# 64 bytes in place of 128 in front of x, g and their sums

## The chip, the core and the metric

The kernel runs on one core of a Trainium2 chip. The metric is the device time of one execution in microseconds (us). One execution was also taken by the profiler; its rows are the evidence for what follows. Engines are named as in the profile: PE is TensorE's matmuls, PEld its weight loads, DVE is VectorE, ACT is ScalarE, SP the engine that issues the transfers.

## What is computed

A pooled attention followed by a feed-forward layer, all in float32. The 576 keys and values of each head are averaged over groups of 8 to 72; eight batches of eight heads with a width of 64 give 4608 tokens of 512 numbers.

```
k_p = k.reshape(B, H, Sp, 8, D).mean(axis=3)      # v_p likewise
scores = q @ k_p.T / sqrt(D);  attn = softmax(scores)
x = (attn @ v_p)  -> (4608, 512)
h = x @ w_in                                       # 512 x 2048
g = max(h, 0) + log1p(exp(-abs(h)))                # softplus
out = g @ w_out                                    # 2048 x 512
```

## The kernel before

The tokens are worked through in 18 chunks of 256 (`CT`). A chunk's attention yields `x`, held as a rounded part `xh` and the rest `xl`, both of type float32r. The weights `w_in` and `w_out` stay in the core's memory (tiles `w0` to `w15`), also as a rounded part and a rest. Each product of two numbers is then three float32r matmuls: high by high, high by low, low by high.

**First product (line 494, `h`).** Per block of 128 columns of `w_in`, 12 matmuls: a 128x128 piece of `w` is loaded as the weights, and 256 tokens of `x` stream through it. In the steady part two blocks (a unit `u` of eight) make 24 matmuls in a row.

**Softplus and its parts.** ACT writes `g` (line 543, 499 in the early chunks) and its rounded part `gh` (557); DVE writes the rest `gl` (564) and, from chunk 4 on, sums of quarters of `g` (594 to 597), which ACT and DVE split into the two halves of `so` (608, 613).

**Second product.** Chunks 0 to 3 accumulate in `acc` (lines 516 and 576): a piece of `gh` or `gl` is the weights and 512 columns of `w` stream. From chunk 4 on (line 684, `m`) seven products take the place of eight: a piece of `gh`, `gl` or `so` is the weights and 256 columns of `w` stream, 21 matmuls a unit. So `x` streams over loads of `w`, and `w` streams over loads of `g`'s parts. The steady part alternates 24 of `h` with 21 of `m`.

The order of all work is written out by a planner in the kernel (`Order`), from costs that the program states; it knows names of slots, not addresses or sizes of tiles. Slots `G0` to `G5`, `o0`, `o1` hold `g`, `sf`, `pm`, output rows and, in chunk 3, `gh` and `gl`, as they come free.

**Where tiles stand.** Tiles of a pool are laid one behind the other in the order in which their tags are first used. `pe` (line 402), the attention weights of the last 8 keys as DVE writes them (line 406), uses `6 * R` of its columns (`R` is 32) and is `7 * R` wide: the last 32 columns, 128 bytes a partition, are never touched. Everything laid behind it is shifted by that width. In the program as built before the change, bytes in a partition:

```
tile (tag)                                  begins   modulo 256   size
vs0, vs1, vlo0, vlo1                          4544 .. 8640     192
w0 .. w15                                  10688 .. 133568   192   8192 each
loads of k, v and weights, q, kp, qT, E     141760 .. 170944   192
G0 (pm, g, sf, o, gh, gl)                   175040             192   2048
pe                                          177088             192    896
lt_, pT                                     177984, 180032      64
x (X01, X23)                                184128, 195904      64   8192 each
gh, gl (two each)                           192320 .. 209216    64   1536 each
so (two)                                    210752, 214848      64   4096 each
G1, G2 and o0, o1, G3 (named by place)      193856 .. 227136    64   2048 each
mn, sm (two each)                           229184 .. 229280    64, 96, 128, 160   32 each
ident                                         1152             128    512
```

All pieces that matmuls read begin a multiple of 512 bytes behind their tile's start, so a tile's phase modulo 256 is that of each of its pieces. `G0` stands ahead of `pe`, the other `G` slots behind it: work in `G0` has the phase of the weights, the same work in another slot the phase of `x`. In unit 3 of chunk 3 the planner put `gh` in `G0` (and `gl` in a slot behind `pe`); in units 0 to 2, 4, 6 and 7 of that chunk both are behind `pe`.

Of the kernel before, what the change touches and what calls it, by code (L numbers as in the profile page):

```python
# [9 lines left out]
F32 = mybir.dt.float32  # L10
# [93 lines left out]
def pooled_attention_softplus_ffn(  # L104
# [14 lines left out]
    P = 128  # L119
# [19 lines left out]
    one = ctx.enter_context(tc.tile_pool(name="one", bufs=1))  # L139
# [157 lines left out]
    R = 4 * KL  # L297
# [31 lines left out]
    class Tile:  # L329
# [69 lines left out]

        def ends(self):  # L400

            pe = one.tile([P, 7 * R], F32, tag="pe", name="pe")
            self.pe = pe[:, 0:6 * R].rearrange("p (a n r) -> p a n r", a=2, n=3)
            for a in range(2):
                hs = slice(4 * a, 4 * a + 4)
                nc.vector.tensor_tensor(  # L406
                    out=self.pe[:, a].rearrange("p n (h j) -> p n h j", h=4),
                    in0=e_[self.c][:, self.t, hs, KM:SP].unsqueeze(1).to_broadcast([P, 3, 4, KL]),
                    in1=self.sm[:, hs].unsqueeze(1).unsqueeze(3).to_broadcast([P, 3, 4, KL]),
                    op=ALU.mult)  # L410
# [539 lines left out]
    def attend(c):  # L950
# [15 lines left out]
        for t, x in enumerate(tiles):  # L966
# [7 lines left out]
            q_free[c, t] = o  # L974
            o = op(ACT, act(512), lambda x=x, s=s_q: x.qT_out(s.tile), [o], [s_q, s_qT])
            ends, ss = [], [Slot("bank"), Slot("bank")]
            p = op(PE, 0.7, lambda x=x, ss=ss: x.scores([bank(s, "sc") for s in ss]), [o, *keys],
                   [s_qT, *ss])
# [18 lines left out]
            if c < N1:  # L997
                exps.extend(ends)
            else:
                subs += ends  # L1000
            norms.append((x, ends, s_E, s_sm, s_pm, s_pe))
        if c == N1:
            ex = op(ACT, 1.2, lambda: exponential(e_[c]), subs, table="exp")
# [386 lines left out]
```

## Time and profile before

| | |
|---|---|
| median of 3 runs | 928.23 us (927.97 to 931.43) |
| the profiled execution | 930.85 us, of which its span 929.1 us |
| PE busy | 904.6 us (97%) |
| PEld busy | 859.6 us |
| DVE, ACT busy | 648.6 us, 407.3 us |
| granted TensorE clock, mean | 0.994 |

The span is from the first instruction to the last. A busy PE says little of its pace, since matmuls overlap and one that takes 281 ns is followed by the next after about 118: the pace of a run is read from the starts of its first matmul and of the next run's first, divided by the count.

### The profile page before, as it was taken

How to read it: one execution, taken by the hardware profiler on the slowest of the kernel's cores; microseconds unless marked ns; L12 is line 12 of the kernel's file. 1: busy time of each engine (PE TensorE's matmuls, PEld its weight loads, DVE VectorE, ACT ScalarE, POOL GpSimd, SP SyncE). 2: the span in 40 equal slices, each digit the busy share in tenths (PEclk: the TensorE clock that was granted, in tenths of full speed). 3: DMA queues.
4: the chain of work that ended last, by engine and by line, in shares of the span. 5: the costliest groups of instructions: out<-in, count | busy, mean ns of one | idle time of the engine just before them, and what ended most of it. 6: DMA issues, size and time to landing. Idle time of an engine off the chain costs nothing.

```text
span 929.1 us, 20504 instructions
## 1 busy us (share of the span) xinstructions
PE 904.6 (97%) x8304; PEld 859.6 (93%) x8304; DVE 648.6 (70%) x1600; ACT 407.3 (44%) x824; POOL 2.4 (0%) x19
## 2 busy tenths in 40 slices
PE   4899999999999999999999999999999999999997
PEld 2678989889899999999999999999999999999997
DVE  4799988868876767777777755777666565747454
ACT  4755433344443534544453435353535344434332
POOL 1000000000000000000000000000000000000000
PEclk9899999999999999999999999999999999999999
DMA  8974636544898678788668865777656566647472
GB/s 231 259 249 147 205 106 182 167 150 136 289 276 239 225 212 256 201 248 233 224 198 248 238 208 186 212 245 214 220 172 216 182 206 186 222 141 227 158 238 78
DMA packets 107085, 191.12 MB, mean 206 GB/s; under 512 B 46064, under 2 KB 60400, under 8 KB 106992
## 3 DMA queue, kind: packets, MB, share of 16 engines
q1 hardware_dynamic: 106992, 189.82, 66.2%
q8 instruction: 65, 1.06, 0.5%
q14 instruction: 28, 0.23, 0.1%
HBM read 167.25 MB, written 22.54 MB: 204 GB/s over the span
## 4 chain that ended last, share of the span: by engine, by line
PE 93%; DVE 3%; DMA 3%; ACT 0%; issue 0%; SPq 0%; DVEq 0%; ACTq 0%
PE h L494 43%; PE m L684 30%; PE acc L516 7%; PE sc L357 3%; PE acc L576 2%; PE avp L461 2%; PE qTp L337 2%; PE avp L468 1%; PE ptp L420 1%; DMA vst<-in_v_dram 1%; PE ltp L432 1%; PE kps L921 1%; DMA kvst<-in_k_dram 1%; DMA kvl<-in_v_dram 1%; DMA wst<-in_moe_w_in_dram 0%
## 5 line engine op out<-in xcount | busy, mean ns | idle before, releaser
L494 PE MATMUL h<-x,w 128*128 128x256 f32 x3456 | 437.8, 282 | 0.7 <-DVE w L822 0.7
L494 PEld LDWEIGHTS h<-x,w 128*128 128x128 f32 x3456 | 422.5, 188 | 4.0 <-DVE w L822 0.9
L543 ACT ACTIVATE g<-h 128x512 f32<-128x512 f32 x120 | 71.7, 598 | 287.0 <-PE h L494 284.7
L684 PE MATMUL m<-w,so 128*128 128x256 f32 x1344 | 177.7, 281 | 0.0
L684 PEld LDWEIGHTS m<-w,so 128*128 128x128 f32 x1344 | 167.4, 188 | 0.0
L684 PE MATMUL m<-w,gh 128*128 128x256 f32 x672 | 133.4, 288 | 0.0
L594 DVE TENSOR_TENSOR sf<-g 128x128 f32<-128x128 f32 x112 | 32.7, 292 | 141.1 <-ACT g L543 140.0
L684 PEld LDWEIGHTS m<-w,gh 128*128 128x128 f32 x672 | 102.2, 188 | 1.9
L684 PE MATMUL m<-w,gl 128*128 128x256 f32 x336 | 94.1, 280 | 0.0
L608 ACT CAST so<-sf 128x512 fp32r<-128x512 f32 x112 | 69.6, 621 | 55.1 <-DVE sf L597 54.6
L613 DVE TENSOR_TENSOR so<-sf,so 128x512 fp32r<-128x512 f32 x112 | 77.3, 690 | 21.9 <-ACT so L608 21.8
L564 DVE TENSOR_TENSOR gl<-g,gh 128x384 fp32r<-128x384 f32 (+1 forms) x120 | 67.3, 560 | 0.7 <-ACT gh L557 0.5
L684 PEld LDWEIGHTS m<-w,gl 128*128 128x128 f32 x336 | 63.1, 188 | 0.0
L516 PE MATMUL acc<-w,g 128*128 128x512 f32 x192 | 60.7, 397 | 0.5 <-ACT g L499 0.5
L557 ACT ACTIVATE gh<-h 128x384 fp32r<-128x384 f32 (+1 forms) x120 | 59.3, 494 | 0.0
L499 ACT ACTIVATE g<-h 128x256 fp32r<-128x256 f32 x96 | 31.6, 382 | 60.7 <-PE h L494 55.6
L705 DVE TENSOR_TENSOR o<-o,m 128x256 f32<-128x256 f32 x98 | 39.7, 418 | 3.9 <-ACT o L697 1.0
L516 PEld LDWEIGHTS acc<-w,g 128*128 128x128 f32 x192 | 34.2, 189 | 6.6 <-ACT g L499 0.7
L364 DVE TENSOR_REDUCE mn<-sc 128x4 f32<-128x288 f32 x72 | 31.1, 450 | 12.2 <-PE sc L357 12.1
L516 PE MATMUL acc<-w,gl 128*128 128x512 f32 x96 | 38.0, 396 | 0.0
L597 DVE TENSOR_TENSOR sf<-g,sf 128x128 f32<-128x128 f32 x112 | 32.7, 292 | 3.9
L406 DVE TENSOR_TENSOR pe<-E,sm 128x96 f32<-128x96 f32 x72 | 15.2, 252 | 26.9 <-PE ltp L432 26.9
(165 smaller groups left out, 933.0 us busy)
## 6 DMA issues: line engine op xcount, KB each, us to landing
w<-wi SPq DMA_DIRECT2D x224, 512.0 KB
out_dram<-o SPq DMA_DIRECT2D x36, 256.0 KB
q<-in_q_dram SPq DMA_DIRECT2D x32, 256.0 KB
wst<-in_moe_w_in_dram SPq DMA_DIRECT2D x32, 256.0 KB
wst<-in_moe_w_out_dram SPq DMA_DIRECT2D x16, 512.0 KB
wi<-w SPq DMA_DIRECT2D x16, 512.0 KB
kst<-in_k_dram SPq DMA_DIRECT2D x24, 288.0 KB
vst<-in_v_dram SPq DMA_DIRECT2D x24, 256.0 KB
```

The lines of the kernel that those rows point to most:

```text
L494: nc.tensor.matmul(out=ps[:, 0:CT], lhsT=row(w, kc), rhs=x[:, kc], start=first and kc == j == 0, stop=last and kc == KC - 1 and j == 2)
L499: nc.scalar.activation(out=g, in_=ps[:, 0:CT], func=AF.Softplus)
L516: nc.tensor.matmul(out=accs[c][t], lhsT=a[:, ts], rhs=w, start=f == 0 and j == 0, stop=f == FC - 1 and j == 2)
L543: nc.scalar.activation(out=g, in_=x.rearrange("p (b i) -> p b i", i=P), func=AF.Softplus)
L557: nc.scalar.activation(out=gh, in_=quarters(c, x.rearrange("p (b i) -> p b i", i=P)), func=AF.Softplus)
L564: nc.vector.tensor_tensor(out=gl, in0=quarters(c, g), in1=gh.bitcast(F32), op=ALU.subtract)
L594: tt(out=sf[:, 2], in0=g[:, 0], in1=g[:, 2], op=ALU.add)
L597: tt(out=sf[:, 3], in0=g[:, 3], in1=sf[:, 1], op=ALU.subtract)
L608: nc.scalar.copy(out=so[:, 0], in_=ss[c, u])
L613: nc.vector.tensor_tensor(out=so[:, 1], in0=sf, in1=so[:, 0].bitcast(F32), op=ALU.subtract)
L684: nc.tensor.matmul(out=ms[c][n], lhsT=x, rhs=y, start=u == 0 and j == 0 and n in (1, 6, 5, 4), stop=u == FP - 1 and j == 2 and n in (2, 7, ...
L705: nc.vector.tensor_tensor(out=o, in0=in0, in1=m[n], op=how)
```

## The change

The tile `pe` is made 6 R + 16 columns wide in place of 7 R: 832 bytes a partition in place of 896, with the used columns as they were.

```diff
         def ends(self):
 
-            pe = one.tile([P, 7 * R], F32, tag="pe", name="pe")
+            pe = one.tile([P, 6 * R + 16], F32, tag="pe", name="pe")
             self.pe = pe[:, 0:6 * R].rearrange("p (a n r) -> p a n r", a=2, n=3)
```

Everything behind `pe` moves down by 64 bytes: `x`, `gh`, `gl`, `so`, `pT`, `lt_` and the `G` slots but `G0` from 64 to 0 modulo 256; `mn` and `sm` from 64, 96, 128, 160 to 0, 32, 64, 96. What stands ahead of it stays, the weights at 192 and `G0` at 192 among it. No instruction is added, removed or resized.

## Rows read from the trace of the kernel before

**Rows 1.** The page: span, busy time of each engine, and the chain that ended last.
```profile
span 929.1 us, 20504 instructions
PE 904.6 (97%) x8304; PEld 859.6 (93%) x8304; DVE 648.6 (70%) x1600; ACT 407.3 (44%) x824; POOL 2.4 (0%) x19
PE 93%; DVE 3%; DMA 3%; ACT 0%; issue 0%; SPq 0%; DVEq 0%; ACTq 0%
```

**Rows 2.** PE's groups by form: line, tiles, shape, count | busy us, mean ns.
```profile
L494 PE MATMUL h<-x,w 128*128 128x256 f32 x3456 | 437.8, 282 | 0.7 <-DVE w L822 0.7
L684 PE MATMUL m<-w,so 128*128 128x256 f32 x1344 | 177.7, 281 | 0.0
L684 PE MATMUL m<-w,gh 128*128 128x256 f32 x672 | 133.4, 288 | 0.0
L684 PE MATMUL m<-w,gl 128*128 128x256 f32 x336 | 94.1, 280 | 0.0
```

**Rows 3.** The chain in order of time: start us, us, what; runs of h, m.
```profile
255.46 2.84 PE h L494 x24
258.30 2.49 PE m L684 x21
260.79 2.84 PE h L494 x24
263.64 2.49 PE m L684 x21
266.13 2.84 PE h L494 x24
```

**Rows 4.** Timeline of PE, chunk 3's unit 3, gh in G0: start us, us, what.
```profile
224.21 0.49 PE L420 MATMUL ptp<-ident,pm 128*128 128x128 f32 x3
224.46 0.71 PE L576 MATMUL acc<-w,gh 128*128 128x512 f32 x2
225.00 0.39 PE L576 MATMUL acc<-w,gl 128*128 128x512 f32 x1
225.23 0.62 PE L576 MATMUL acc<-w,gh 128*128 128x512 f32 x2
...
227.07 0.40 PE L576 MATMUL acc<-w,gl 128*128 128x512 f32 x1
227.31 0.27 PE L432 MATMUL ltp<-ident,pe 128*96 128x128 f32 x1
```

**Rows 5.** Timeline of PE, chunk 3's unit 7, gh and gl behind pe.
```profile
252.51 0.63 PE L576 MATMUL acc<-w,gh 128*128 128x512 f32 x2
252.97 0.39 PE L576 MATMUL acc<-w,gl 128*128 128x512 f32 x1
...
255.30 0.75 PE L494 MATMUL h<-x,w 128*128 128x256 f32 x5
```

**Rows 6.** Timeline of PE: first and last of the 73 joins m to h.
```profile
260.51 0.28 PE L684 MATMUL m<-w,gl 128*128 128x256 f32 x1
260.63 0.63 PE L494 MATMUL h<-x,w 128*128 128x256 f32 x4
...
916.18 0.28 PE L684 MATMUL m<-w,gl 128*128 128x256 f32 x1
916.30 0.51 PE L494 MATMUL h<-x,w 128*128 128x256 f32 x3
```

**Rows 7.** Weight loads by form, and transposes by line: durations min/median/max.
```profile
L684 PEld LDWEIGHTS m<-w,so x1344: 187/188/193, 258.7 to 923.6; 128*128 128x128 f32 x192
L420 PEld LDWEIGHTS ptp<-ident,pm x144: 138/141/143, 31.2 to 860.6; 128*128 128x128 f32 x144
L420 PE MATMUL ptp<-ident,pm x144: 271/272/328, 31.7 to 860.7; 128*128 128x128 f32 x144
```

**Rows 8.** DVE and ACT lines on g, in G0 or behind pe: durations min/median/max.
```profile
L594 DVE TENSOR_TENSOR sf<-g x112: 281/292/295, 253.3 to 920.0; 128x128 f32<-128x128 f32 x112
L543 ACT ACTIVATE g<-h x120: 597/598/603, 200.4 to 919.3; 128x512 f32<-128x512 f32 x120
L608 ACT CAST so<-sf x112: 619/621/640, 255.1 to 921.1; 128x512 fp32r<-128x512 f32 x112
L397 DVE TENSOR_TENSOR pm<-E,sm x36: 637/682/694, 20.6 to 857.5; 128x512 f32<-128x512 f32 x36
```

**Rows 9.** PE's waits: line, releaser: us in total, times, longest.
```profile
PE kps L921 <- DVE kvst L914: 6.0, 1, 6.0
PE ltp L432 <- DVE pe L406: 4.8, 4, 1.5
```

**Rows 10.** Timeline of the end: the last matmuls, DVE's last sums and the last output.
```profile
923.98 2.00 DVE L705 TENSOR_TENSOR o<-o,m 128x256 f32<-128x256 f32 x5
924.03 0.28 PE L684 MATMUL m<-w,gl 128*128 128x256 f32 x1
925.22 1.12 SPq L528 DMA_DIRECT2D out_dram<-o  x2
```

## The prediction

> **What bounds the kernel now.** I read the page first: PE is busy for 904.6 of the 929.1 us of the span, and the chain that ended last lies on PE for 93% [rows 1]. Then PE's groups: 3456 matmuls of `h` and 1344 + 672 + 336 = 2352 of `m`, all 128x256 in float32r [rows 2]. Their busy time is no pace, since they overlap; the chain in order of time gives it. A run of 24 `h` takes 2.84 us, 118.3 ns each, a run of 21 `m` 2.49 us, 118.6 ns [rows 3]. So 5808 matmuls x 118.45 ns = 688 us, 74% of the span, are two alternating streams at one pace. The 384 matmuls of `acc` stream 512 columns at about 232 ns (below), another 89 us. PE's waits come to a few us, the longest ones in the first stage and behind `pe` [rows 9]. A change of place can only matter if it alters those two paces, or lengthens DVE or ACT so far that PE waits for them.
>
> Is there something to gain or lose in the pace? Transposes, with 128 float32 columns of `ident` over loads of the same 128x128 size, follow each other at (490 - 272) / 2 = 109 ns [rows 4, 7]. So 118.45 isn't the shortest step seen; 9.45 ns a matmul, 55 us in all, lie between. The weight loads differ too: 188 ns in the float32r products, 141 in the transposes [rows 7].
>
> **The change part by part.** No instruction comes or goes, no wait, no transfer; the planner sees neither sizes nor addresses, so the order on each engine stays. `pe` itself begins where it did. Only phases move. There are four kinds of users.
>
> 1. *Stream against weight load.* While one matmul streams, the next one's weights are read. Today `x` (64) streams over loads of `w` (192), and `w` over loads of `g`'s parts (64): 128 apart both times. After: `h` at +64, `m` and `acc` at -64 modulo 256. No float32r row of before stands at 64 apart, so I bound it from rows at 0 and 128.
>  (a) In chunk 3's unit 3 `gh` lies in `G0`, so 8 of its 12 loads are at distance 0 under streams of `w`. From the second matmul to the transpose behind the unit are 11 steps, 7 of them over loads of `gh` at distance 0: 227.31 less 224.46 is 2.85 us, of which the first step, which waited, is 0.31 (the row of two begins at 224.46, lasts 0.71 and its second matmul 0.40 or a little less, so that one starts at 224.77). 2.54 us / 11 = 230.9 ns [rows 4]. In unit 7, with 11 of 12 loads at distance 128, 2.79 us / 12 = 232.5 ns [rows 5]. Distance 0 is no slower by these rows: -1.6 ns, with rows given to 10 ns (1 ns a step).
>  (b) Where `m` ends and `h` begins, `w` streams over a load of `w`: one load at distance 0. The step is 0.12 us at the first and the last of the 73 joins [rows 6]; read to the ns the 73 average 121.3. That is 1.6 (by the rows) to 2.8 ns above 118.45. But a run with such a step at its head has no longer sum: 21 `m` at 118.6 and 24 `h` at 118.3 hold one each [rows 3], so the extra is given back in the steps behind it, or isn't the phase's doing.
>  (c) The load's own time is 187 to 193 ns in all 1344 loads of `so` [rows 7], with no second group.
>  So the price of 0 against 128 lies between -1.6 and +2.8 ns a matmul. For 64 apart I take 0: nearest to (a) and to the sums in [rows 3], which hold whole runs. There is a reason too why one distance should do as another. A load of 512 bytes lasts 47 ns longer than a transpose's [rows 7]; if that is because it is read at half the speed, it is read for some 94 ns (an estimate), 5.4 bytes a ns, while the stream passes 1024 bytes in at most 118 ns, 8.7 a ns. The stream then gains about 310 bytes on the load, more than 256: it passes every phase at least once wherever it begins.
>
>  The row (a) shows no price. [...]
>
> 2. *DVE and ACT.* Lines 594, 543 and 608 work in `G0` (192) in some units and behind `pe` (64) in the others; across both their durations are 281/292/295, 597/598/603 and 619/621/640 ns [rows 8]. So 128 bytes cost at most 3 ns in a few hundred; I take 0 for 64. Line 397 spreads from 637 to 694 [rows 8], and its `sm` moves from 128 and 160 to 32 and 64: either way 36 x 0.05 us = 1.8 us of DVE time, beside PE. PE waited 4.8 us for `pe`, 4 times [rows 9]; each of those could move by 0.05, 0.2 us in all.
>
> 3. *Transposes and scores.* `pm` is transposed from `G0` and from slots behind `pe`; the 144 loads take 138 to 143 ns and the matmuls a median of 272 [rows 7]. Cost 0.
>
> 4. *Transfers.* Output rows begin at 0 in place of 64 in the slots behind `pe`. Only the last one is on the path: issued from 925.22, landed by 929.1 [rows 10]. Perhaps 0.2 us either way.
>
> The sum: 5808 x 0 + 384 x 0, plus or minus 0.4. The profiled execution's 930.85 us stays what it is; it stood 2.6 above the median of 928.23, inside the runs' own range, so I forecast **928.2**. What a measurement of this kernel can tell from no change is about 0.5%, 4.6 us, or 0.8 ns a matmul in 5808.
>
> **The rivals.**
>
> *Slower: the two streams do collide, and 64 lies nearer to the collision than 128.* Place: every float32r load of `h` and `m`. Price: what a load at distance 0 shows at the joins, 1.6 to 2.8 ns [rows 3, 6], so 9.3 to 16.3 us: 937.5 to 944.5. It decides if a collision reaches 64 bytes but not 128, and if the extra of the joins isn't given back when it comes at every step. For it: the first and the last of the joins, 656 us apart, show the same step. Against: (a), and the sums in [rows 3]. Price at half reach: 4.6 us, just at the bound of what can be told.
>
> *Faster: the period is 128, so 0 and 128 look alike, and 64 is the one place not seen yet.* Then today's streams meet at the same phase, and 64 would keep them apart for part of a load. The far end is the transposes' step: 55 us for `h` and `m` [rows 3, 4], 873. As the stream passes the load's phase anyway, I take a quarter: 13.7 us, 914.5. For it: (a) finds 0 and 128 alike, and 118.45 has 9.45 ns over the shortest step that no wait explains. Against: the load takes longer by itself in float32r [rows 7], which explains the step without any collision. The same mechanism could have the other sign; that is in the slower rival's chance.
>
> *It does not do what it says.* If tiles were laid to multiples of 128, `x` would not move. `mn` and `sm` stand 32 bytes apart, and 832 is 26 x 32, so they do move; and then it would be 928.2 all the same.
>
> **How the numbers follow.** No change by any of the ways above: 0.60, and its own range is 925 to 932 (the spread of the runs and 2 us of small terms on either side). Slower by the collision: 0.22, most of it between 933 and 945. Faster by the period: 0.18, from just under 924 down to 873, half of it above 915. For 8 in 10 I leave out the lower half of the faster case (0.09) and the upper third of the slower one (0.07): 915 to 940. Beyond 0.5%: faster 0.18, same 0.60, slower 0.22.
>
> **What would show it.** After the change a run of 24 `h` and one of 21 `m` should again take 2.84 and 2.49 us. If the collision is real, both grow, to 2.88 and 2.53 at least; if only one of them moves, the sign of the distance (+64 for `h`, -64 for `m`) matters, which no part here has allowed for. Loads should stay at 188 ns; if they change, the load and not the stream is what the phase acts on. Units of chunk 3 with `gh` behind `pe` stand at -64, that with `gh` in `G0` still at 0: their steps against 232.5 and 230.9 test (a) at 512 columns. DVE's line 594 should keep its 292. I'd be wrong if a pace changes by 0.8 ns or more, or if PE gets new waits for DVE while its pace stays.

## The result, and the profile after

The changed kernel takes 917.24 us (three runs, 915.2 to 918.51) against 928.23: a ratio of 0.9868 [0.9834, 0.9901], 1.3% faster. The time lies inside the range, but the likeliest case, no change, was wrong. The profiled executions took 915.2 and 930.85 us, with spans of 913.5 and 929.1 at the same mean granted clock of 0.994, so the two traces can be set side by side. They differ by 15.6 us, the medians by 11.0: the profiled execution stood 2.6 us above its median before and 2.0 below it after.

The page after: span, and busy time of each engine, as in [rows 1]:

```profile
span 913.5 us, 20504 instructions
PE 888.3 (97%) x8304; PEld 842.9 (92%) x8304; DVE 648.7 (71%) x1600; ACT 407.3 (45%) x824; POOL 2.4 (0%) x19
```

The count of instructions is the same, and DVE and ACT are busy for as long as before. PE lost 16.3 us. Its groups by form, as in [rows 2] (line, tiles, shape, count | busy us, mean ns):

```profile
L494 PE MATMUL h<-x,w 128*128 128x256 f32 x3456 | 430.2, 279 | 0.7 <-DVE w L822 0.7
L684 PE MATMUL m<-w,so 128*128 128x256 f32 x1344 | 172.6, 278 | 0.0
L684 PE MATMUL m<-w,gh 128*128 128x256 f32 x672 | 131.9, 285 | 0.0
L684 PE MATMUL m<-w,gl 128*128 128x256 f32 x336 | 93.7, 279 | 0.0
```

`h` and `m` gave 7.6 + 5.1 + 1.5 + 0.4 us of busy time, nearly all of it. The chain in order of time shows how (start us, us, what), as in [rows 3]:

```profile
253.95 2.82 PE h L494 x24
256.77 2.40 PE m L684 x21
259.17 2.72 PE h L494 x24
261.89 2.48 PE m L684 x21
264.37 2.83 PE h L494 x24
267.19 2.39 PE m L684 x21
```

Where every run of `h` took 2.84 us and every run of `m` 2.49 [rows 3], there are now two lengths of each: 2.83 and 2.72, 2.48 and 2.40. The reader is to see that no run is a mixture. Read from the starts of single matmuls, a run goes through at 113, 113, 114 ns, over and over, or at 117 to 119 ns, mean 117.9, from its first few steps to its last. Of the runs behind 256 us, 47 of 110 of `h` and 74 of 111 of `m` are of the short kind. Before there was one pace with a beat of five steps (122, 120, 119, 115, 118).

Over all steps without a stall the means are 116.35 ns for `h` (118.56 before) and 115.28 for `m` (118.49). 3456 x 2.21 = 7.6 and 2352 x 3.21 = 7.5 us: 15.2 of the 15.6 us between the spans. The 384 matmuls of `acc` went from 232.4 to 233.4 ns, which takes back 0.4.

PE's waits for DVE are what they were [rows 9]; the one behind `pe` (line, releaser: us in total, times, longest):

```profile
PE ltp L432 <- DVE pe L406: 4.9, 4, 1.5
```

### The profile page after: what moved, and what is told of

Read it like the earlier page. It is cut to its first block, busy times and chain, and to the rows that moved or that the text cites. A ratio compares the mean times of both kernels' runs of the same rounds, so it can differ in the third digit from the quotient of the medians.

```text
span 913.5 us, 20504 instructions
## 1 busy us (share of the span) xinstructions
PE 888.3 (97%) x8304; PEld 842.9 (92%) x8304; DVE 648.7 (71%) x1600; ACT 407.3 (45%) x824; POOL 2.4 (0%) x19
## 4 chain that ended last, share of the span: by engine, by line
PE 94%; DVE 3%; DMA 1%; ACT 0%; issue 0%; SPq 0%; DVEq 0%; ACTq 0%
PE h L494 43%; PE m L684 30%; PE acc L516 7%; PE sc L357 3%; PE acc L576 3%; PE avp L461 2%; PE qTp L337 2%; PE avp L468 1%; PE ptp L420 1%; PE ltp L432 1%; DMA kvst<-in_k_dram 1%; PE kps L921 1%; DMA kvl<-in_v_dram 1%; DVE pm L397 0%; PE kvlp L880 0%
## 5 line engine op out<-in xcount | busy, mean ns | idle before, releaser
L494 PE MATMUL h<-x,w 128*128 128x256 f32 x3456 | 430.2, 279 | 0.7 <-DVE w L822 0.7
L494 PEld LDWEIGHTS h<-x,w 128*128 128x128 f32 x3456 | 414.9, 188 | 4.1 <-DVE w L822 0.9
L684 PE MATMUL m<-w,so 128*128 128x256 f32 x1344 | 172.6, 278 | 0.0
L684 PEld LDWEIGHTS m<-w,so 128*128 128x128 f32 x1344 | 162.6, 188 | 0.0
L406 DVE TENSOR_TENSOR pe<-E,sm 128x96 f32<-128x96 f32 x72 | 15.2, 253 | 25.8 <-PE ltp L432 25.8
```

The costliest lines, as they stand in the source:

```text
L494: nc.tensor.matmul(out=ps[:, 0:CT], lhsT=row(w, kc), rhs=x[:, kc], start=first and kc == j == 0, stop=last and kc == KC - 1 and j == 2)
L684: nc.tensor.matmul(out=ms[c][n], lhsT=x, rhs=y, start=u == 0 and j == 0 and n in (1, 6, 5, 4), stop=u == FP - 1 and j == 2 and n in (2, 7, ...
```

## The experiments

Below, the *distance* is the place where the streamed operand starts less the place where the weights loaded under it start, modulo 256 bytes. Before: 128 for `h` and for `m`. After: 64 for `h`, 192 (which is -64) for `m`. A *step* is the time from the start of one matmul to that of the next of the same line, steps with a stall (over 140 ns) left out; a run's length in the chain over its count gives it to half a ns. Each ratio is against runs of the kernel before on the same chip in the same session.

### Four other rooms

One number changes; 0, 32, 96 and 160 bytes of room:

```diff
-            pe = one.tile([P, 7 * R], F32, tag="pe", name="pe")
+            pe = one.tile([P, 6 * R], F32, tag="pe", name="pe")        # s0: distances 0 and 0
+            pe = one.tile([P, 6 * R + 8], F32, tag="pe", name="pe")    # s32: 32 and 224
+            pe = one.tile([P, 6 * R + 24], F32, tag="pe", name="pe")   # s96: 96 and 160
+            pe = one.tile([P, 6 * R + 40], F32, tag="pe", name="pe")   # s160: 160 and 96
```

> pe 6 R wide: x, g and their sums begin at 192 modulo 256, the weights' own phase (distance 0). Theory D (the distance between the streamed operand and the weights loaded under it sets the pace of float32r matmuls): a third pace beside 118.6 ns (distance 128) and the mix of 113.4 and 117.9 ns (distance 64); from the joins of before, 120.1 to 121.3 ns, so 937 to 945 us. Theory A (only where x and g themselves begin counts, and 0 modulo 256 is the good place): 192 is as bad as 64 was, pace 118.6, 928 us. Theory S (the 16-us gain came from a few places such as the joins or chunk 3): 928 us or less.

> 32 bytes of room: x and g at 224, distance 32. Theory D: between distance 0 and 64; with the period of 128 that the rival of the prediction named, no slower than distance 64, 905 to 917 us; if the meeting of the two reads reaches 64 bytes, 917 to 945. Theory A: not at 0 modulo 256, pace 118.6, 928 us.

> 96 bytes of room: x and g at 32, distance 96. Theory D: between distance 64 (917 us) and 128 (928 us). Theory A: 928 us. If what counts is that x begins at a multiple of 64, it is slower than 928.

> 160 bytes of room: x and g at 96, distance 160, that is 96 the other way round. Since h and m have opposite signs of the distance, theory D without a sign gives the same time as 96 bytes of room, 917 to 928 us; with a sign, the paces of h and m change places against 96. Theory A: 928 us.

| room | distance h, m | step h, m (ns) | time (us) | ratio |
|---|---|---|---|---|
| 0 | 0, 0 | 119.80, 119.78 | 934.97 | 1.0059 [1.0028, 1.0091] |
| 32 | 32, 224 | 117.02, 118.24 | 926.34 | 0.9950 [0.9921, 0.9979] |
| 64 (after) | 64, 192 | 116.35, 115.28 | 917.24 | 0.9868 [0.9834, 0.9901] |
| 96 | 96, 160 | 119.85, 118.27 | 933.46 | 1.0028 [1.0005, 1.0050] |
| 128 (before) | 128, 128 | 118.56, 118.49 | 928.23 | 1 |
| 160 | 160, 96 | 118.04, 119.87 | 930.61 | 1.0010 [0.9983, 1.0036] |

In the session of rooms 0, 32, 96 and 160 the kernel before took 930.15 us; 917.24 and 928.23 are from the session of the result. Room 0 is slower, as theory D said, but by less than its 937 to 945 us. Room 32 lies in theory D's wider range. Room 96 is slower than either theory had it. At 160 the paces of `h` and `m` change places against 96, as theory D with a sign had it. Theory A's one pace of 118.6 ns came in none of the four, theory S's 928 us or less fails at room 0, and the guess that `x` should begin at a multiple of 64 fails at room 32, which is faster with `x` at 224.

Runs in the chain in order of time: first of room 0, then of room 96, then of room 160.

```profile
259.19 2.88 PE h L494 x24
262.07 2.52 PE m L684 x21
```

```profile
259.19 2.88 PE h L494 x24
262.06 2.49 PE m L684 x21
```

```profile
259.84 2.82 PE h L494 x24
262.66 2.52 PE m L684 x21
```

`h` at 96 and `m` at 96 have the same step (119.85 and 119.87 ns), and so nearly have `h` and `m` at 160 (118.04 and 118.27), though the two streams differ in what they read and the distance changed sign between them. So at these distances the step is one function of the signed distance, and no smooth one: 0 and 96 are the slowest, and 64 lies between them. At distance 0 the weight loads too take longer, 191 to 192 ns against 188 to 190 in the other rooms. That isn't what makes the step long: at 96 it is as long with loads of 188 (`h`) and 189 to 190 ns (`m`). The largest group of loads in room 0 (line, tiles, shape, count | busy us, mean ns | idle us before):

```profile
L494 PEld LDWEIGHTS h<-x,w 128*128 128x128 f32 x3456 | 426.5, 192 | 3.7 <-DVE w L822 0.9 <-issue 0.2
```

### All of it 64 bytes further

The changed kernel, with 64 bytes ahead of every tile. The distances stay, and every tile starts elsewhere modulo 256:

```diff
+    const.tile([P, 16], F32, name="room")
     ident = const.tile([P, P], F32, name="ident")
```

> The kernel after with 64 bytes of room ahead of everything: weights at 0, x and g at 64 modulo 256, as x and g were before, distance 64 as after. Theory D: as the kernel after, 917 us, h at 116.3 and m at 115.3 ns. Theory A (x and g beginning at 0 modulo 256 is what helps): 928 us, 118.6 ns.

Measured: 913.17 us, 0.9822 [0.9797, 0.9847], with steps of 116.35 and 115.34 ns, those of after. (The time is 4.1 us below that of after, measured in another session; with equal steps, that difference isn't theirs.) Runs in the chain in order of time:

```profile
255.98 2.72 PE h L495 x24
258.70 2.48 PE m L685 x21
261.18 2.83 PE h L495 x24
264.01 2.40 PE m L685 x21
```

It is the distance and not the place at which `x` and `g` begin; the theory that wanted them at a multiple of 256 falls.

### The distance alone, with nothing else running

A kernel of 96 units of 48 matmuls with line 494's operands (the rest of the computation is left out), executed once: distance 0 to 248 upward and down again in steps of 8, then distances 0, 64, 128 and 192, each with both operands moved together by 0, 32, ... 224 bytes.

```diff
+    plan = [(0, d) for d in range(0, 64, 2)]
+    plan += [(0, d) for d in range(62, -2, -2)]
+    plan += [(s, d) for d in (0, 16, 32, 48) for s in range(0, 64, 8)]
```

> This kernel leaves the whole computation out and runs the disputed pair alone: units of 96 float32r matmuls as in line 494 (load 128x128, stream 256 columns), no other engine at work, no wait between units. The stream begins 0, 8, ... 248 bytes from the weights modulo 256, then the same downwards, then distances 0, 64, 128 and 192 with both operands shifted by 0, 32, ... 224. Theory D: the pace depends on the distance as in the whole kernel (0: 119.8 ns, 32: 117.0, 64: 113.4 or 117.9, 96: 119.9, 128: 118.6, 160: 118.1, 192: 113.4 or 117.9, 224: 118.2), the same for every common shift. Theory A (the start of x itself): the pace follows the shift. Theory E (DVE, ACT or transfers collide with TensorE's reads, and the phase only moves that): one pace near 113 ns for all units, since nothing else runs.

The stretches of the four distances moved together, then distance 64 on the way up and on the way down. Columns: us, its length, PE's busy us (matmuls under way in it, about three more than start in it), granted clock, DMA share, GB/s.

```profile
381.60:421.60 40.00, 40.00 (x336) 1.00 0.01 1
427.50:467.10 39.60, 39.60 (x339) 1.00 0.00 1
472.80:512.60 39.80, 39.80 (x338) 1.00 0.01 1
518.30:557.90 39.60, 39.60 (x338) 1.00 0.00 1
55.70:61.10 5.40, 5.40 (x50) 1.00 0.00 0
324.40:329.80 5.40, 5.40 (x48) 1.00 0.00 0
```

The granted clock is 1.00 in all of them. DVE's copies end before PE begins at 8.61 us and its next one starts at 558.12, ACT has no work, and the DMA share is 0.01 at most: other engines and transfers aren't needed for the effect. Mean steps of the units, read from the starts, the first four steps of each unit left out:

| distance | ns a step (up / down, where they differ) |
|---|---|
| 0 | 120.0 (the first unit, behind PE's idle 8.61 us, left out: the execution's mean granted clock is 0.979) |
| 16, 32, 48 | 116.7 / 118.7, 116.7, 118.4 / 118.3 |
| 64 | 113.3 / 117.8 |
| 80, 96, 112 | 120.0 / 118.3, 120.0, 114.1 (113.3 after about a dozen steps) |
| 128, 144, 160, 176 | 118.7 / 118.6, 118.7, 117.3 / 117.4, 119.3 |
| 192 | 113.3 / 117.8 |
| 208, 224, 240 | 119.0, 118.3, 117.1 |
| odd multiples of 8 | 118.3 to 122.8, most at 120.0 |

Moving both operands together leaves 120.0 at 0, 117.8 at 64 and 192, and 118.6 to 118.8 at 128, also where `x`, to stay inside its tile, is put back by 256 bytes and the weights are not. So the period is 256 or a part of it, and as 0 and 128 differ it is not 128 or less: 256. At 64 and 192 the same distance has two steady paces: 113.3 on the way up, 117.8 on the way down and in all sixteen units later. What differs is what came before. The tile that takes the products alternates from unit to unit, and the sixteen later units are long with either, so that isn't what selects the pace.

### x alone, g alone

```diff
+    rooms = ctx.enter_context(tc.tile_pool(name="rooms", bufs=1))      # x_only: h 64, m 128
+    rooms.tile([128, 16], F32, name="room")
+    xpool = ctx.enter_context(tc.tile_pool(name="xpool", bufs=1))
...
+    xpool = ctx.enter_context(tc.tile_pool(name="xpool", bufs=1))      # g_only: h 128, m 192,
+    two = ctx.enter_context(tc.tile_pool(name="two", bufs=2))          # both ahead of wpool
...
-            x = one.tile([P, 2, HP, CT], F32R, tag={"a": "X01", "b": "X23"}[name or "ab"[c % N1]],
+            x = xpool.tile([P, 2, HP, CT], F32R, tag={"a": "X01", "b": "X23"}[name or "ab"[c % N1]],
...
+            pe = one.tile([P, 6 * R + 16], F32, tag="pe", name="pe")   # both
```

> The x tiles of chunks 0, 1 and 3 to 17 stand behind the weights with 64 bytes of room, all the rest as before the change: x streams 64 from the weights (h at distance 64, as after), w streams 128 from g's parts (m at distance 128, as before). Theory D: h takes after's mix of 113.3 and 117.9 ns, mean near 116.3, m stays at 118.5: 3456 x 2.2 ns = 7.6 us less, about 921 us. If x alone made the gain: 915 to 917 us. If g's parts alone made it: 928 us.

> The counterpart: x stays 128 from the weights (h at distance 128), g's parts and sums come to 64 from them as after (m at distance 192). Theory D: h stays at 118.5 ns, m takes after's mix, mean near 115.3: 2352 x 3.2 ns = 7.5 us less, about 921 us. If x alone made the gain: 928 us. If g alone: 915 to 917 us.

`x` alone: 925.99 us, 0.9952 [0.9937, 0.9968], steps 117.84 and 118.71. `g` alone: 925.56 us, 0.9958 [0.9940, 0.9976], steps 118.44 and 116.20. Neither reaches the 921 us that theory D gave each. Against 929.96 in their session that is 4.0 and 4.4 us, 8.4 together; the two at once gave 11.0 (after) and 16.9 (all 64 bytes further). The intervals of the times are too wide to settle it alone. The steps settle it: by the same working as for the result they are worth 2.0 and 5.8 us, 7.8 together, against 15.2 for the two at once. (About half of what `x` alone gained lies outside these steps. By the order of the pools the tiles between `w` and `pe`, `G0` among them, moved by 64 bytes in that kernel too.) The chain in order of time, `x` alone, then `g` alone:

```profile
257.77 2.83 PE h L497 x24
260.60 2.49 PE m L687 x21
```

```profile
255.03 2.39 PE m L685 x21
257.42 2.84 PE h L495 x24
```

With `m` at 128 beside it, `h` at 64 takes its long pace nearly every time, while after it has 2.72 in every second run of this stretch: behind 256 us 1 of 110 runs is short, against 47. With `h` at 128, `m` at 192 is short in none of the 55 runs that follow `h` directly, and in 46 of the 55 that follow other work of PE. So the parts don't add up, because each stream's pace depends on the other's distance as well: what a run inherits where it joins the run before decides which of its paces it takes.

### Alternating runs, all pairs of distances

24 matmuls of `h` and 21 of `m` in turn, six times over for each of 64 pairs of distances in steps of 32 bytes (the rest of the computation is left out), with four transposes at three places, executed once. Then the same in steps of 16 for `m`, with `h` at 112, 64, 192, 16, 240 and 32.

```diff
+    for a in range(0, 64, 8):               # turns16: for a in (28, 16, 48, 4, 60, 8):
+        for b in range(0, 64, 8):           #              for b in range(0, 64, 4):
+            for i in range(6):
+                if i in (3, 5):
+                    turn(ts)
+                h(a, hs[0])
+                if i == 4:
+                    turn(ts)
+                m(b, hs[1])
```

> This kernel leaves the computation out: runs of 24 matmuls as in line 494 and 21 as in line 684 in turn, 6 turns for each of 64 pairs of distances (h: 0, 32, ... 224; m the same), with four transposes let in before the fourth and sixth run of h and the fifth run of m. Theory D: a run's pace depends on its own distance, 0: 120, 128: 118.7; at 64 and 192 it is either 113.3 or 117.8 ns all through a run. Theory J (what the run inherits at the join decides between the two): at h 64 and m 192 the fast and the slow pace change at each join of h to m and stay at each join of m to h, as in the kernel after; at h 64 and m 64, or 192 and 192, they do not change, so that some pair of distances is fast all through, mean 113.3 to 114 ns. Theory R (chance decides): each run fast or slow without order.

> As the kernel of turns, the computation left out, now in steps of 16 bytes: h at 112, 64, 192, 16, 240, 32, each with m at 0, 16, ... 240; 24 of h and 21 of m in turn, with transposes let in. Theory J (a run at 64 or 192 is fast or slow all through, by what it takes over at the join): the same two paces as before. In the run of pairs, distance 112 came to 113.3 ns from both sides within a dozen matmuls: if it does so whatever goes before (theory F), h at 112 takes 113.3 to 114.5 ns in nearly every run, whatever m's distance, and m at 112 the same, so that 112 for both is the best pair, under 114.5 ns; if it was entered by luck there, its runs split into two paces as at 64 and 192, mean 115 to 117 ns.

The chain in order of time, at (0, 0), at (64, 64), at (64, 192) and at (192, 32); L43 is `h`, L52 is `m`:

```profile
16.74 2.88 PE h L43 x24
19.62 2.52 PE h L52 x21
...
612.05 2.83 PE h L43 x24
614.87 2.47 PE h L52 x21
...
744.63 2.72 PE h L43 x24
747.35 2.48 PE h L52 x21
749.82 2.83 PE h L43 x24
752.65 2.40 PE h L52 x21
755.49 2.83 PE h L43 x24
758.32 2.40 PE h L52 x21
...
1642.11 2.75 PE h L43 x24
1644.86 2.46 PE h L52 x21
```

(0, 0) repeats room 0's 2.88 and 2.52. At (64, 192) the two lengths of the changed kernel return, in its order: short `h`, long `m`, long `h`, short `m`. The pace changes where `m` follows `h` and stays where `h` follows `m`; between 752.65 and 755.49 transposes lie at the join, and `h` is long behind them. The same holds after: of the joins `h` to `m` with neither a wait nor other work of PE between, all 55 change the pace, and of those from `m` to `h` all 73 keep it. So chance (theory R) is out. At (64, 64) all runs are long; at (192, 192) `h` goes at about 114 ns and `m` at 117.7. Theory J had expected no change at either pair, and so one that is fast all through; there is none. It isn't enough that each distance has a short pace.

Over a whole pair, transposes included, the mean is least at (192, 32) with 120.4 ns and at (64, 192) and (192, 64) with 120.5; (0, 0), with its runs of 2.88 and 2.52 us, is near the other end. In steps of 16 it is (192, 32) again, 120.3. Counting only the runs that follow one another directly, the changed kernel's own pair (64, 192) is least in both kernels, 114.9 ns against 115.4 at (192, 32). The distance 112, which had been fast from both sides in the sweep, reached 113.3 for `h` in most runs only after nine to fifteen steps (the runs straight behind `m` have means of 113.4 to 119.5 ns, most near 115.4), and not for `m`, whose runs went at 117 to 120.2. That it would do for both was wrong, and no pair clearly better than the changed kernel's turned up.

### The two best pairs in the kernel

```diff
+    two = ctx.enter_context(tc.tile_pool(name="two", bufs=2))
+    rooms = ctx.enter_context(tc.tile_pool(name="rooms", bufs=1))
+    rooms.tile([128, 16], F32, name="room")
+    xpool = ctx.enter_context(tc.tile_pool(name="xpool", bufs=1))
...
+            pe = one.tile([P, 6 * R + 8], F32, tag="pe", name="pe")    # h192_m32
+            pe = one.tile([P, 6 * R], F32, tag="pe", name="pe")        # h192_m64
```

> The whole kernel with x at 192 from the weights and the weights at 32 from g's parts (the two distances with the lowest mean in the run of turns). Theory D with the paces of turns (h 113.7, m 116.7 ns): 3456 x 4.9 + 2352 x 1.8 = 21 us less than before, 909 us, against 917 after. If stalls at the joins decide more than the distance (turns has few), h splits into 113.3 and 117.8 as after: 915 to 920 us.

> The mirror image of the change: x at 192 from the weights, the weights at 64 from g's parts. Theory D without more: as after, 917 us. Theory J: the paces of turns (h 115.7, m 114.8 ns): 3456 x 2.9 + 2352 x 3.7 = 18.7 us less than before, 911 us; and h and m change places against after, where m is fast more often than h behind a stall: which of the two is fast behind a stall shows whether the sign of the distance or the kind of run decides.

(192, 32): 914.45 us, 0.9830 [0.9804, 0.9856], steps 115.00 and 116.86; 93 of 109 runs of `h` are short. (192, 64): 917.20 us, 0.9859 [0.9830, 0.9888], steps 115.90 and 116.04. Their chains in order of time:

```profile
256.03 2.75 PE h L497 x24
258.77 2.46 PE m L687 x21
```

```profile
256.35 2.83 PE h L497 x24
259.18 2.47 PE m L687 x21
261.65 2.73 PE h L497 x24
264.39 2.38 PE m L687 x21
```

At (192, 64), the changed kernel's pair mirrored, the joins are mirrored too: the pace now changes where `h` follows `m` (all 72 without a stall) and stays where `m` follows `h` (all 55). The sign of the distance decides at which join it changes. Where a wait or other work of PE lies between, the order is looser, but it is mirrored as well: after, 3 of 37 such runs of `h` are short and 48 of 55 of `m`; here 24 of 37 of `h` and 14 of 55 of `m`. The stream at 192 is the faster one both times, so there too it is the sign and not the kind of run.

At (192, 32) `m` met its price of 116.7 ns, but `h` did not go at 113.7: it averages 114.5 behind 256 us, where 16 of its 109 runs are long, and about 117 in the first three chunks. So 914.45 came in place of 909 us. (192, 64) gave the 917 of theory D and not the 911 by the paces of the alternating runs. The ratio of (192, 64) lies within the changed kernel's interval; 0.9830 is just below it (from 0.9834), but within that of the changed kernel 64 bytes further (from 0.9797). So neither is a better version that these runs can tell from it.

## Why the prediction was wrong though its range held, point by point

The range, 915 to 940 us, holds 917.24, but by luck. Its main case was no change, and its lower end was the middle of the faster rival, whose reason turned out wrong (below).

*What bounds the kernel* was right: PE alone, by the two alternating streams, and between the two traces the span moved by nearly what their steps moved (15.2 of 15.6 us).

*Part 1* is the step that failed: 0 ns for 64 apart, in place of -2.2 (`h`) and -3.2 (`m`). Three things went into that 0.

First, bound (a). The row [rows 4] is right and came back: after, the unit with `gh` in `G0` is still at distance 0, and its eleven steps run from 223.37 to 225.91, 230.9 ns again. PE's timeline of its head and end:

```profile
223.06 0.71 PE L576 MATMUL acc<-w,gh 128*128 128x512 f32 x2
...
225.91 0.38 PE L432 MATMUL ltp<-ident,pe 128*96 128x128 f32 x2
```

But it says nothing of matmuls half as wide. With 512 columns distance 0 is the quickest of these (`acc`: 229.5 ns in room 0, 232.4 at 128, 233.4 at 192); with 256 columns it is among the slowest (119.8). I let a row of one form of matmul set the price for another, in the form where 5808 and not 384 are at stake.

Second, bound (b) was the better one: 1.6 to 2.8 ns at a join, and room 0 costs 1.24 and 1.29 ns at every step (7.3 us by the steps; its median is 4.8 us above 930.15). The same trace held a second such row that I did not read: where `h` ends and `m` begins, `x` streams over a load of `gh`, also at distance 0, and the 56 such steps without a wait average 120.1 ns. That the sums of whole runs hid it [rows 3] was no argument: each held one such step in 21 or 24.

Third, the reason. I held that a stream which gains 310 bytes on the load passes every phase wherever it begins, so that one distance does as another. The 310 were my estimate, from a load read at half the speed, which no run shows. The runs show steady patterns instead, 113, 113, 114 at one distance and a beat of five steps at another, and the distance goes with the pattern. I read them as load and stream locked to each other; no run shows it. The prices at 0 and 128 could not bound a third place either, as the jagged table shows: 64 is better than both. The range between -1.6 and +2.8 ns had no reason behind it beyond two points.

With no other engine at work these float32r pairs took 113.3 to 122.8 ns a step, by the distance and by what ran before. Whether it is the reads themselves that get in each other's way, no run shows.

*Parts 2 to 4* were right. DVE's line 594 takes 293 ns in place of 292, line 397 684 in place of 682, and the transposes' loads stay at 138 to 144 ns [rows 7, 8]. The last output row is issued at 909.64 us, 3.9 before the end, as before [rows 10]. By line, durations min/median/max, after:

```profile
L594 DVE TENSOR_TENSOR sf<-g x112: 284/293/295, 251.8 to 904.4; 128x128 f32<-128x128 f32 x112
L397 DVE TENSOR_TENSOR pm<-E,sm x36: 639/684/695, 20.9 to 843.4; 128x512 f32<-128x512 f32 x36
L420 PEld LDWEIGHTS ptp<-ident,pm x144: 138/140/144, 30.6 to 846.3; 128*128 128x128 f32 x144
```

*The rivals.* The faster one gave 914.5 and 917.24 came, but its reason was wrong: 0 and 128 are not alike (119.8 and 118.56 ns in the kernel), the period isn't 128, and the quarter of 55 us was a choice. What it had right is that 64 was a place not yet seen. The slower one's longer step is real at distance 0 and, as large, at 96; its premise that nearness to 0 decides is not. *It does not do what it says* is out by room 32 and room 96, where `x` moves by 32 bytes and the steps change.

*What would show it* put the finger on the gap: "the sign of the distance matters, which no part here has allowed for". It matters, not by giving `h` and `m` two prices at 64 and 192, which have the same two paces, but by deciding at which join a run changes from one to the other. Its own sign of being wrong, a pace that changes by 0.8 ns or more, came true. The chances were the deeper fault: with no row at 64 and a price known to differ between 0 and the rest, 0.60 for no change was too much.

What stays open: why these distances and not others, whether and where the two reads meet, and what behind a stall or other work decides between the two paces. That a run inherits its pace at the join is shown by the sequences; how it is carried over isn't.

## What to carry to other kernels

Where a chain of float32r load and matmul pairs sets the time, look at the steady step over whole runs, and ask where streamed operand and weights start modulo 256 bytes: a few spare bytes ahead of a tile moved this step here, with 256 columns, between 113 and 120 ns. Don't price such a place from its neighbours, or from matmuls of another width; measure a sweep with a bare kernel, then the runs in the order in which the kernel alternates them, since a pace here depended on the run before (after, all 55 direct joins of `h` to `m` changed it). The gains of the parts of such a change need not add up: here they were 7.8 us by the steps, against 15.2 for the two at once.

## What the runs showed of the hardware that I had not expected

- The step of a float32r matmul of 256 columns with a load of 128x128 under it is a jagged function of the distance modulo 256 bytes, 113.3 to 122.8 ns with no other engine at work, at a granted clock of 1.00 and a DMA share of 0.01 at most in the stretches read.
- At 64 and at 192 bytes the same stream has two steady paces, 113.3 and 117.8 ns, and goes on at the one that it has: in the sweep all sixteen later units at these distances went at 117.8.
- The shortest steady step seen for this pair is 113.3 ns, not the 109 of the float32 transposes, by which I had set the far end of the faster rival.
- At distance 0 the weight loads lengthen from 188 to 192 ns together with the step; at 96 the step is as long with loads of 188 to 190.
